# One PSUM pool of eight single banks, halves apart, and a new written order, in a memory-attention and spatial-gate kernel

## The chip, the cores and the metric

The kernel runs on one core of a Trainium2 chip. Its time is the device time of one execution in microseconds (us), the median of three runs. TensorE (PE in the profile) multiplies matrices and writes the products to PSUM, a memory of eight banks of 128 partitions by 512 fp32 values; VectorE (DVE) and ScalarE (ACT) read PSUM and write SBUF; GpSimd (POOL) works in SBUF alone; SyncE (SP) issues all DMA transfers here.

## The reference

For each of 8 batches (8 heads, 576 rows, 64 columns, 32 memories), `_attn_ref` makes memories out of the keys and values and lets the queries attend to them; `_moe_ref` puts the result through a gated layer whose gate mixes rows.

```python
a = softmax(phi)                                  # (b, h, 576, 32), over the memories
k_m, v_m = a^T k, a^T v                           # (b, h, 32, 64)
attn = softmax(q k_m^T / 8)                       # (b, h, 576, 32)
x = concat_heads(attn v_m)                        # (b, 576, 512)
h = relu(x w_in); u, v = halves of h              # 512 columns each
v_n = (v - mean) / sqrt(var + 1e-6)               # over the columns
v_s = w_spatial v_n + b_spatial[:, None]          # mixes the 576 rows
out = (u * v_s) w_out                             # (b, 576, 512)
```

`w_in` and `w_out` arrive in double precision, as pairs of 32-bit words that the kernel decodes.

## The kernel before, in words

Products that must be exact to fp32 are made of fp32r operands in two parts: a value x becomes hi = fp32r(x) and lo = x - hi, and a product is hi*hi + hi*lo + lo*hi, three matmuls. The low part is made by `low`: either DVE subtracts hi from x in PSUM, or PE adds minus hi onto x in its bank and ACT copies the rest out. ON_VECTOR names the ones that DVE makes; "wtl0" is one of them.

Each stage of a batch is a Python generator that yields after one or a few instructions, and each has a letter. P: exp(phi) and its sum (`memory_weights`). K: memories (`memories`, tiles kvm, tk, tv). Q: queries loaded and transposed. S: scores and their softmax (`scores`, tile sc, four banks). M0, M1: value memories times a half of w_in (`products`, tile mp, cast to mh and ml). V0 to V4: the gate half v of a tile of 128 rows (the last has 64), normalised (`gate`, tile pv). U0 to U3: the half u, transposed, for 128 of its 512 columns (`units`, tile pu, then one ACT Relu into u). G0 to G3: the row mixing for 128 columns (`spatial`, tile ps, 28 matmuls; then DVE multiplies by u into g, and ACT and DVE split g into gh, gl and the last 64 rows into grh, grl). O0 to O4: output rows (`project`, tile po, 12 matmuls, an ACT copy, a DMA). Once at the start: D loads w_in, E and L decode its two halves, X loads and decodes w_out, W loads w_spatial, T0 to T4 transpose it (tile wt), B adds the bias, and Z is an idle matmul that only keeps PE busy.

Nothing schedules these at run time. START, PLAN and END are strings of such letters, written by hand: each letter runs its generator up to its next yield, so the strings give the order of instructions on every engine and on every DMA queue. A prime means one batch ahead. START runs batch 0 and the first stages of batches 1 and 2, PLAN is walked for batches 1 to 5, END runs the last two. Each engine runs its own list in order and waits on the others by semaphores. A tile is given a bank of its pool when its first instruction is written, and where all banks of the pool are taken, that instruction waits for the last reader of the tile that gives way.

Before, PSUM is two pools: ps1, four single banks (`bank`), for mt, mb, kvm, tk, tv, sc, pv, po, tq, at and the idle matmuls; and ps2, two tiles of two banks each (`banks`), for wt, mp, pu and ps. So two of M, U, G can be in flight, and the third waits until the whole of a two-bank tile is read. A batch takes 9 to 10 two-bank tiles and some 19 single ones.

Of the kernel before, what the change touches and what calls it, by code (L numbers as in the profile page):

```python
# [26 lines left out]
    P'' G1 Q' K' V4 V3 X1 V2 V4 G1 G2*2 Q' V3 G2 K' V3 V4*2 P'' V3 K'*2 P'' G2 X1 Q' K' P'' G2
    X1 X3 P'' K'' G2 K' X2 G2 K'' K' G1 P'' X3 P'' X3 P'' G1 X3 G0 G1 G0 G1 K' G1*2 G0 P''*2 G0
    X2 G3 G2 K' P'' G3 X2 G2 S' M1' X2 G0 X2 P'' G3 G0*2 S'*2 O0 P'' X2 X3 G3 X2 X3 S' O2 X3 S'
    M1'*2 S' G3 G0 O3 G3 G0 G3 S' M1' O3 O1 S'*2 O3 P'' O1 P'' S' Q'' O1 S' G3 M1' S' G3 O0 S'  # L30
    O3 O2 S' M1' S' O0 S'*5 O2 K'' O0 K'' Q'' O2 O1 K''*2
# [6 lines left out]
    M1' K'' G1 S' G0 G1 P''' G0 S'*2 G1 G3 O1 S' G2 G1 S' M0 S' P''' G3 S'*2 G3 G0 G3 G2 O0 G3*2
    S'*2 G2 Q'' O2 G2 S' V1' G2 O1 V0' O3 V1' O1 V1' P''' O1 G2 O0 O1 V0' M1 O0 G2 K'' U3' Q''
    S' O3 V0' V4' O2 P''' Q'' O4 K'' Q'' O3 V4' O0 O4 V4' U1'*2 P''' O2 V4' O4 O2 O4 O0 V4' P'''  # L40
    K'' Q'' K''' O3
# [3 lines left out]
    V0 V1 V4 V1 V0 V1 K' U3*2 V0 V2 V0 U2 V2 U1 U2 V1 V3 V2*2 U2 V2 V3 U0*2 M0' U0 M1' Q' S' V4  # L45
    M0' V3 G1 M0'*2 M1' G1 V3 M0' M1'*2 V3 G0 M1' V2 V4 S' V2 V3 G0 G1 V4 S' G0 S'*2 V3 V4 S' G0
    S' G0 S' G1 G3 G0 G1 G0 S' G3 G1 G3 S' G3 S'*2 U1 G2 S' G2 G0 G1 G0 V4 G2*2 S'*3 G1 O3 S' G1
    G3 U1' S'*2 V0' V2' S' V1' G2 V0' U1' V1' U1' V0' O0 U0' O2 U0' U3' V2' G2 V3' U0' G3 V4 G2
    V1' V2' V0'*2 G3 O2 G2 V0' U2' V2' U2' V0' O0 V2' U3' U2' G3*2 V1' G0' V4' V1' V3' O3 V2'
    V1' V3' V1' V4' O0 G0' V3' V4' U3' G1' V3' V4' V2' V3' V4' O1 Q' G0' G2 G1' V3' V4'*2 O1 V4'  # L50
    Q' G1' O3 V4'*2 G1'*3 G0' G2' G1' G2'*2 G1' G0' G2' G0' G3' G0'*2 O1 G3' G0' G3'*2 O2 O0 O1'
    G3' O1 G3' G1' G2'*2 O4' O3' G2' O2 O0' G2' G3' O1'*3 O0' O3' G3' V4 O3' O3 O3' G2' G3' K'
    O0' O4' O0' O2' O4' O2'*2 O4' O2'
# [838 lines left out]
```

## Time and profile before

| | before |
|---|---|
| median of 3 runs | 436.64 us (435.97 to 437.99) |
| profiled execution, its own time | 436.06 us |
| its span, first to last instruction | 434.3 us |
| PE, DVE, ACT, POOL busy | 405.9, 275.1, 230.6, 102.5 us |
| matmuls | 3882 |

A profile of one execution gives each instruction's start and length on its engine, the idle time before it, and the engine that ended this idle time. The ends of matmuls are modelled and overlap the next one's start, so two neighbouring starts tell more of PE's rate than a length. PEld is the weight load, which runs beside PE. An idle time is put down to the releaser that came last.

### The profile page before, as it was taken

Reading aid. Unit: us, or ns where it says so; the run is one execution under the profiler, and the core shown is the slowest. Engines: PE = TensorE matmul, PEld = TensorE weight load, DVE = VectorE, ACT = ScalarE, POOL = GpSimd, SP = SyncE. Lnnn points to the kernel's source line nnn. Section 1 sums busy time; section 2 is a strip of 40 time slices with the busy share of each in tenths; the row PEclk is TensorE's granted clock in tenths of the full one; section 3 lists DMA queues with packets and bytes.
Section 4 is the critical chain, followed back from the end, with each engine's and each line's share of the span. In section 5 each row is a group of like instructions: output and inputs, shape, how many; then the busy total and the mean of one; then the engine's idle time right before and its main releaser. Section 6 shows DMA issues by size and latency. Waiting matters only on the chain.

```text
span 434.3 us, 9318 instructions
## 1 busy us (share of the span) xinstructions
PE 405.9 (93%) x3882; PEld 344.1 (79%) x3882; DVE 275.1 (63%) x492; ACT 230.6 (53%) x444; POOL 102.5 (24%) x191
## 2 busy tenths in 40 slices
...
GB/s 305 365 381 249 74 76 207 146 27 250 150 208 12 105 163 129 110 26 154 83 219 2 103 183 160 60 54 142 121 2 2 127 51 2 0 2 24 2 48 145
DMA packets 85725, 50.68 MB, mean 117 GB/s; under 512 B 66162, under 2 KB 70258, under 8 KB 85684
## 3 DMA queue, kind: packets, MB, share of 16 engines
...
q14 instruction: 11, 0.09, 0.1%
...
## 4 chain that ended last, share of the span: by engine, by line
PE 47%; DVE 20%; ACT 14%; DMA 8%; POOL 5%; issue 4%; SPq 1%; POOLq 0%; DVEq 0%; ACTq 0%
PE po L798 18%; PE ps L758 14%; PE pv L636 6%; PE pu L720 4%; ACT vr L693 4%; DMA raw<-in_moe_w_in_dram 3%; DVE ml L153 3%; DVE vl L698 3%; DVE rmx L553 2%; DVE sm L556 2%; ACT mh L612 2%; DMA out_dram<-o 2%; ACT vh L696 2%; DVE phi_sb L311 2%; DMA q_sb<-in_q_dram 1%
## 5 line engine op out<-in xcount | busy, mean ns | idle before, releaser
L758 PE MATMUL ps<-wth,vh 128*128 128x288 f32 x256 | 57.3, 305 | 7.4 <-DVE ml L153 4.1
L758 PE MATMUL ps<-wtl,vh 128*128 128x288 f32 x256 | 54.6, 294 | 0.0
L758 PE MATMUL ps<-wth,vl 128*128 128x288 f32 x256 | 54.5, 294 | 0.0
L758 PEld LDWEIGHTS ps<-wth,vh 128*128 128x128 f32 x256 | 40.8, 188 | 13.1 <-issue 4.4
L798 PE MATMUL po<-woh,gh 128*128 128x512 f32 x128 | 50.4, 394 | 0.2 <-DVE sm L547 0.2
L798 PE MATMUL po<-wol,gh 128*128 128x512 f32 x128 | 50.3, 393 | 0.0
L798 PE MATMUL po<-woh,gl 128*128 128x512 f32 x128 | 50.2, 392 | 0.0
L804 ACT COPY o<-po 128x512 f32<-128x512 f32 x36 | 21.1, 585 | 46.1 <-PE po L798 35.1
L758 PEld LDWEIGHTS ps<-wtl,vh 128*128 128x128 f32 x256 | 41.4, 188 | 0.0
L758 PEld LDWEIGHTS ps<-wth,vl 128*128 128x128 f32 x256 | 40.9, 188 | 0.0
L681 DVE BATCH_NORM_STATS2 st<-vr 128x6 f32<-128x512 f32 (+1 forms) x35 | 24.0, 684 | 22.9 <-ACT vr L678 22.8
L684 POOL TENSOR_SCALAR few<-few 128x1 f32<-128x1 f32 (+1 forms) x35 | 9.7, 276 | 120.1 <-DVE few L682 105.3
L693 ACT ACTIVATE vr<-vr,few 128x512 f32<-128x512 f32 (+1 forms) x40 | 32.5, 815 | 8.9 <-POOL few L688 8.9
L586 POOL CAST ar<-ah 128x128 fp32r<-128x128 f32 x7 | 6.1, 874 | 130.2 <-ACT ah L579 130.2
L433 DVE STREAM_TRANSPOSE qT<-q_sb 128x576 f32<-128x576 f32 x28 | 20.2, 753 | 23.6 <-DMA q_sb<-in_q_dram 19.0
L698 DVE TENSOR_TENSOR vl<-vr,vh 128x512 fp32r<-128x512 f32 x32 | 22.0, 691 | 20.5 <-ACT vh L696 19.6
L720 PE MATMUL pu<-ah,mh 128*128 128x288 f32 x128 | 28.9, 307 | 0.1
L579 ACT CAST ah<-aT 128x576 fp32r<-128x576 f32 x14 | 9.4, 675 | 36.3 <-DVE aT L575 36.3
L798 PEld LDWEIGHTS po<-woh,gl 128*128 128x128 f32 x128 | 24.1, 188 | 5.5
L153 DVE TENSOR_TENSOR ml<-mp,mh 128x512 fp32r<-128x512 f32 x28 | 18.8, 688 | 15.1 <-ACT mh L612 15.1
L798 PEld LDWEIGHTS po<-woh,gh 128*128 128x128 f32 x128 | 24.1, 188 | 5.1 <-issue 0.4
L720 PE MATMUL pu<-ah,ml 128*128 128x288 f32 x128 | 27.4, 296 | 0.4 <-ACT ml L151 0.4
...
## 6 DMA issues: line engine op xcount, KB each, us to landing
...
```

The lines of the kernel that those rows point to most:

```text
L153: nc.vector.tensor_tensor(lo, x, hi.bitcast(F32), op=ALU.subtract)
L433: nc.vector.transpose(qT[:, 2 * n : 2 * n + 2].rearrange("p h s -> p (h s)"), q_sb[:, 2 * n : 2 * n + 2].rearrange("p h i d -> p (h i d)"),)
L579: nc.scalar.copy(ah[:, r], aT[:, r])
L636: nc.tensor.matmul(pv, x[:, r, cs], m[:, r, DM:DFF], start=(n == 0), stop=(n == 5))
L681: nc.vector.bn_stats(st6, vr)
L684: nc.gpsimd.tensor_scalar_add(rs, mv[:, 1:2], 1e-6)
L693: nc.scalar.activation(vr, vr, AF.Identity, bias=sh, scale=rs)
L698: nc.vector.tensor_tensor(vl[:, st, :], vr, vh[:, st, :].bitcast(F32), op=ALU.subtract)
L720: nc.tensor.matmul(pu[:, hf, 0:HALF], m[:, r, cs], a[:, r, hf * HALF : (hf + 1) * HALF], start=(n == 0), stop=(n == 5),)
L758: nc.tensor.matmul(ps[:, hf, 0:HALF], a, w[:, hf * HALF : (hf + 1) * HALF], start=(n == 0), stop=(n == len(ops) - 1),)
L798: nc.tensor.matmul(po, a, w, start=(n == 0), stop=(n == 11))
L804: nc.scalar.copy(o, po)
```

## The change

- ps1 has eight single banks and ps2 is gone. The tiles pu, ps and mp become two single tiles each; the 576 columns of pu and ps stay cut in halves of 288.
- `units` runs its matmuls half by half (three for the first half, three for the second, in each of its two steps), and two Relu of 288 columns take the place of one of 576.
- `spatial` multiplies g in two halves, two DVE instructions in place of one.
- `transpose_spatial` has a tile for 512 columns and one for 64; each is cast and has its low part made apart. The names become wtl00, wtl01 and so on, so none is in ON_VECTOR: PE and ACT make the low part of tile 0 too.
- The tiles grh and grl are kept under the number of the pair of batches.
- START, PLAN and END are new throughout. In START w_spatial is loaded ahead of w_in, both pieces of w_in's second half ahead of its first half, and there are 29 idle matmuls where there were 25.

The diff; of the three strings the parts that the text below speaks of are shown.

```diff
--- before.py
+++ after.py
@@ -18,39 +18,41 @@
 PSUM = bass.MemoryType.PSUM
 
 START = """
-    P Z P*2 Z P*2 Q P*9 Q P Q P Q K Q*4 K Q*2 P Z Q Z Q Z D1 K W E0 K W K*2 Z D0 K*2 E0*2 Z K*4
-    S Z S K S*2 W S T1 D1 Z L0 S*2 T1 D0 Z X0 T4 Z T3 Z T3 S T1 S X1 T1 S E1 Z E0 S*3 Z T4 Z T4
-    T3 L0 Z S*2 L1 T3 E1 S Z T4 Z*2 T0 S E1 S T4 X1 Z E1 T0 S L0 L1 T0 S*2 Z M1*2 S*2 X1 L0 L1
...
+    P Q*2 Z P*2 K P*2 Q*2 P Q P*2 Q*2 P K Q P*2 Q*2 P Z Q P*4 K P K Q K*2 W K*3 Z*2 W K Z K T4 K
+    T0 D1 S T1 K D1 S D0 E0 Z T0 S*2 T0*2 S E0 S*2 T0 E0 Z W T1 S T1 Z*2 X0 D0 T4 Z T1 Z E1 Z E1
+    S T0 Z*2 S Z E0 Z*2 T3 Z T1 S T4 E1 X0 T1 S T3 L0 Z*2 E1 T4 T0 Z L1 L0 Z T1 S L1 L0 S T4 S
+    P' Z T3 S M1 X1 T3 Z T4 S M1 T3 T4 S*2 X1 Z*2 S*2 M1*2 X1 L1 T2 S*2 L0 L1 P' Z M1 T2 Z S Z
+    T2 S*3 M1 M0 T4 P' T2 V0 P' S P' X0 T2*2 M0 P' M0 T2 X0 P' V0 M0 P' M0 Q' V1 K' V0 V2 M0 V0
...
 """
 
 PLAN = """
-    M0 V0 V4 V1 V0 U1 U3 V2 V0 U3 U0 K' U0 V1*2 Q' P'' V2 V3 P'' V4 V0 V1 P'' U2*2 V3 S' V2*2 U0
-    M0' M1' V3 S' S S' P'' U2 P''*2 V2 K'' M0'*2 V3 M0'*2 M1'*2 K'' G1 M1' V3 G1 V2 V4 P'' M1'
-    P'' K''' S' G0*2 V3 V2 V4*2 G1 V3 P''' G0 S' G0 S' G1 G3 K'' S' G0 G3 S' G3 G0 G2*2 G1 K''*3
...
+    M0 V1 V4 V0 U0 V3 V1 K' V0 U0 V1 U1 P'' U3 U2 Q' U2 M1 V0 Q' P'' V1 V2 V0 U2*2 V3 U0 P'' S'
+    M0' V2 P'' V3 V2 S' V3 S' P'' V2 S' K'' P'' S' M0'*2 P'' M0' P'' M0' M0 V4 S' V3 M1' K''
+    G0*2 V2*2 V4 V3 G1 K'' V2 V3 P''' M1' V4*2 G1 M1' S' G1*2 S' G1 G0 K''' S G0 K'' P'''*2 G3
...
 """
 
 END = """
...
 """
 
 ON_VECTOR = set(
@@ -93,14 +95,10 @@
     one = ctx.enter_context(tc.tile_pool(name="one", bufs=1))
     three = ctx.enter_context(tc.tile_pool(name="three", bufs=3))
     two = ctx.enter_context(tc.tile_pool(name="two", bufs=2))
-    ps1 = ctx.enter_context(tc.tile_pool(name="ps1", bufs=4, space=PSUM))
-    ps2 = ctx.enter_context(tc.tile_pool(name="ps2", bufs=2, space=PSUM))
+    ps1 = ctx.enter_context(tc.tile_pool(name="ps1", bufs=8, space=PSUM))
 
     def bank(name):
         return ps1.tile([P, 512], F32, tag="b1", name=name)
-
-    def banks(name):
-        return ps2.tile([P, 2, 512], F32, tag="b2", name=name)
 
     ident = const.tile([P, P], F32, name="ident")
     make_identity(nc, ident)
@@ -234,14 +232,14 @@
             nc.gpsimd.tensor_copy(w_dup, w_sb[:, :, None, SM:S].to_broadcast([P, NI, 2, SR]))
             nc.gpsimd.tensor_copy(w_rem_dup, w_rem[:, None, SM:S].to_broadcast([SR, 2, SR]))
             yield
-        tp = banks(f"wt_{si}")
+        tp, tr = bank(f"wt_{si}"), bank(f"wr_{si}")
         for ti in range(NI + 1):
             if si < NI:
                 cols = (w_rem if ti == NI else w_sb[:, ti])[:, si * P : (si + 1) * P]
             else:
                 cols = (w_rem_dup if ti == NI else w_dup[:, ti]).rearrange("t c s -> t (c s)")
             n = cols.shape[0]
-            dst = tp[:, 0, ti * P : ti * P + n] if ti < NI else tp[:, 1, 0:n]
+            dst = tp[:, ti * P : ti * P + n] if ti < NI else tr[:, 0:n]
 
             nc.tensor.matmul(
                 dst,
@@ -252,14 +250,12 @@
                 stop=ti >= NI - 1,
             )
         yield
-        x = tp.rearrange("p a s -> p (a s)")[:, 0:S]
         hi = wth[:, si] if si < NI else ws1
-        nc.scalar.copy(hi, x)
-        yield
-        if si < NI:
-            yield from low(f"wtl{si}", wtl[:, si], x, hi)
-        else:
-            yield from low(f"wtl{si}", ws2[0:SR], x[0:SR], hi[0:SR])
+        lo, n = (wtl[:, si], P) if si < NI else (ws2[0:SR], SR)
+        for c, (cs, x) in enumerate(((slice(0, SM), tp), (slice(SM, S), tr[:, 0:SR]))):
+            nc.scalar.copy(hi[:, cs], x)
+            yield
+            yield from low(f"wtl{si}{c}", lo[:, cs], x[0:n], hi[0:n, cs])
 
     def prepare_bias(b, _):
 
@@ -596,8 +592,7 @@
         vT = state["vT", b]
 
         cs = slice(f * 512, (f + 1) * 512)
-        both = banks(f"mp_{b}_{f}")
-        mps = [both[:, r] for r in range(2)]
+        mps = [bank(f"mp_{b}_{f}_{r}") for r in range(2)]
         for j in range(NJ):
             for r in range(2):
                 nc.tensor.matmul(
@@ -711,25 +706,23 @@
             state["u", b] = one.tile([P, NJ, S], F32, name="u")
         u = state["u", b]
         (ah, al, _), (mh, ml) = state["a", b], state["m", b]
-        pu = banks(f"pu_{b}_{dt}")
         cs = slice(dt * P, (dt + 1) * P)
-        n = 0
+        pu = [bank(f"pu_{b}_{dt}_{hf}")[:, 0:HALF] for hf in range(2)]
+        at = [slice(hf * HALF, (hf + 1) * HALF) for hf in range(2)]
         for r in range(2):
-            for m, a in ((mh, ah), (mh, al), (ml, ah)):
-                for hf in range(2):
+            for hf in range(2):
+                for n, (m, a) in enumerate(((mh, ah), (mh, al), (ml, ah))):
                     nc.tensor.matmul(
-                        pu[:, hf, 0:HALF],
+                        pu[hf],
                         m[:, r, cs],
-                        a[:, r, hf * HALF : (hf + 1) * HALF],
-                        start=(n == 0),
-                        stop=(n == 5),
+                        a[:, r, at[hf]],
+                        start=(r == 0 and n == 0),
+                        stop=(r == 1 and n == 2),
                     )
-                n += 1
-            yield
-        nc.scalar.activation(
-            u[:, dt, :].rearrange("p (a s) -> p a s", a=2), pu[:, :, 0:HALF], AF.Relu
-        )
-        yield
+            yield
+        for hf in range(2):
+            nc.scalar.activation(u[:, dt, at[hf]], pu[hf], AF.Relu)
+            yield
 
     def spatial(b, dt):
         if ("g", b) not in state:
@@ -737,13 +730,13 @@
                 one.tile([P, NJ, SM], F32R, name=name) for name in ("gh", "gl")
             )
             if b % 2 == 0:
-                state["rem"] = tuple(
+                state["rem", b // 2] = tuple(
                     one.tile([P, NJ, 2 * SR], F32R, name=name) for name in ("grh", "grl")
                 )
-        u, (gh, gl), (grh, grl) = state["u", b], state["g", b], state["rem"]
+        u, (gh, gl), (grh, grl) = state["u", b], state["g", b], state["rem", b // 2]
         vh, vl, t1 = state["v", b]
         rc = slice((b % 2) * SR, (b % 2 + 1) * SR)
-        ps = banks(f"ps_{b}_{dt}")
+        ps = [bank(f"ps_{b}_{dt}_{hf}")[:, 0:HALF] for hf in range(2)]
         cs = slice(dt * P, (dt + 1) * P)
         ops = []
         for i in range(NI):
@@ -756,7 +749,7 @@
         for n, (a, w) in enumerate(ops):
             for hf in range(2):
                 nc.tensor.matmul(
-                    ps[:, hf, 0:HALF],
+                    ps[hf],
                     a,
                     w[:, hf * HALF : (hf + 1) * HALF],
                     start=(n == 0),
@@ -766,13 +759,10 @@
                 yield
         yield
         g = two.tile([P, S], F32, name="g")
-        nc.vector.tensor_tensor(
-            g.rearrange("p (a s) -> p a s", a=2),
-            u[:, dt, :].rearrange("p (a s) -> p a s", a=2),
-            ps[:, :, 0:HALF],
-            op=ALU.mult,
-        )
-        yield
+        for hf in range(2):
+            at = slice(hf * HALF, (hf + 1) * HALF)
+            nc.vector.tensor_tensor(g[:, at], u[:, dt, at], ps[hf], op=ALU.mult)
+            yield
         for hi, lo, x in (
             (gh[:, dt, :], gl[:, dt, :], g[:, 0:SM]),
             (grh[:, dt, rc], grl[:, dt, rc], g[:, SM:S]),
@@ -792,7 +782,7 @@
             if st < NI:
                 h_, l_ = (x[:, dt, st * P : (st + 1) * P] for x in state["g", b])
             else:
-                h_, l_ = (x[:, dt, :] for x in state["rem"])
+                h_, l_ = (x[:, dt, :] for x in state["rem", b // 2])
             woh, wol = (x[:, dt % 2] for x in state["wo", dt // 2])
             for a, w in ((h_, woh), (h_, wol), (l_, woh)):
                 nc.tensor.matmul(po, a, w, start=(n == 0), stop=(n == 11))
```

## Rows read from the trace of the kernel before

**Rows 1.** The page's part 1: busy time of an engine, its share of the span, and its instructions.

```profile
PE 405.9 (93%) x3882; PEld 344.1 (79%) x3882; DVE 275.1 (63%) x492; ACT 230.6 (53%) x444; POOL 102.5 (24%) x191
```

**Rows 2.** Busy time by stretch: from and to, its length, then busy time and instructions of PE, PEld, DVE, ACT and POOL, the granted clock of PE as a share of 2.4 GHz, the DMA engines' busy share and GB/s.

```profile
44.00:47.70 3.70, 3.52 (x20) 1.49 (x21) 2.93 (x5) 2.01 (x5) 2.47 (x3) 0.54 1.58 146
47.70:102.00 54.30, 52.56 (x616) 43.79 (x614) 37.26 (x65) 36.24 (x76) 19.03 (x35) 1.00 0.40 105
...
128.65:177.90 49.25, 48.01 (x464) 41.59 (x464) 32.84 (x61) 25.83 (x50) 9.62 (x21) 1.00 0.48 114
177.90:225.10 47.20, 45.38 (x452) 39.16 (x452) 32.64 (x61) 25.00 (x49) 10.22 (x21) 1.00 0.50 109
...
321.40:370.20 48.80, 46.04 (x317) 39.06 (x317) 29.99 (x55) 24.12 (x48) 6.78 (x17) 1.00 0.21 40
370.20:416.80 46.60, 46.53 (x293) 42.95 (x294) 22.54 (x43) 20.93 (x40) 8.55 (x17) 1.00 0.05 18
```

**Rows 3.** What PE waited for in the whole span: the tile it was to write or read and its line, the releaser, us in total, how often, the longest.

```profile
PE ps L758 <- DVE ml L153: 4.1, 5, 1.3
PE mt L296 <- DVE mx L283: 3.9, 2, 3.6
PE ps L758 <- DVE g L769: 2.7, 6, 0.9
...
PE mb L305 <- ACT cmb L302: 2.2, 3, 0.8
...
PE pv L636 <- ACT vr L678: 1.1, 1, 1.1
...
PE mp L603 <- DVE g L769: 0.6, 1, 0.6
...
PE mp L603 <- ACT u L729: 0.4, 1, 0.4
PE pv L644 <- ACT o L804: 0.3, 1, 0.3
PE po L798 <- DVE sm L547: 0.2, 1, 0.2
```

**Rows 4.** PE's timeline at one batch boundary: start, length, line, tile and operands, shape, how many in a row, and the idle time before it with its releaser.

```profile
211.03 1.20 PE L536 MATMUL sc<-qT,kT 64*32 64x288 f32 x32
212.03 2.05 PE L603 MATMUL mp<-win_sb,vT 64*32 64x512 f32 x32
213.87 2.22 PE L338 MATMUL kvm<-kv_sb,phi_sb 64*32 64x128 f32 x144
216.73 0.51 PE L758 MATMUL ps<-wth,vh 128*128 128x288 f32 x2 [0.64 <-DVE ml L153]
...
224.04 0.69 PE L758 MATMUL ps<-ws,t 128*128 128x288 f32 x4
225.09 0.53 PE L758 MATMUL ps<-wth,vh 128*128 128x288 f32 x2 [0.35 <-DVE g L769]
```

**Rows 5.** The end of the chain of waits: start, length, and so many matmuls in a row.

```profile
405.95 10.84 PE ps L758 x82
416.79 13.74 PE po L798 x60
```

**Rows 6.** Instructions grouped by line and form: engine, operation, tile, shape, count, busy us and mean ns of one, and the idle time before them.

```profile
L769 DVE TENSOR_TENSOR g<-u,ps 128x576 f32<-128x576 f32 x32 | 23.2, 742 | 5.7 <-PE ps L758 5.5
L782 DVE TENSOR_TENSOR gl<-g,gh 128x512 fp32r<-128x512 f32 x32 | 22.2, 708 | 8.3 <-ACT gh L780 8.2
L729 ACT ACTIVATE u<-pu 128x576 f32<-128x576 f32 x32 | 20.5, 644 | 5.1 <-PE pu L720 4.9
L678 ACT ACTIVATE vr<-pv 128x512 f32<-128x512 f32 x28 | 16.6, 594 | 18.6 <-PE pv L636 17.5 <-DVE vl L698 1.1
L547 DVE STREAM_TRANSPOSE sm<-sc 128x288 f32<-128x288 f32 x28 | 12.2, 460 | 0.0
L681 DVE BATCH_NORM_STATS2 st<-vr 128x6 f32<-128x512 f32 x28 | 19.2, 684 | 17.0 <-ACT vr L678 16.9
L782 DVE TENSOR_TENSOR grl<-g,grh 128x64 fp32r<-128x64 f32 x32 | 6.7, 208 | 8.9 <-ACT grh L780 8.9
L311 DVE TENSOR_TENSOR phi_sb<-phi_sb,mb 128x1152 f32<-128x1152 f32 x7 | 9.5, 1352 | 3.2 <-PE mb L305 3.2
L383 ACT COPY vT<-tv 128x128 f32<-128x128 f32 x8 | 2.1, 264 | 0.0
```

**Rows 7.** GpSimd's timeline in the start: the decoding of w_in and what it waits for.

```profile
17.32 2.89 POOL L178 TENSOR_SCALAR raw<-raw 128x1024 int32<-128x1024 uint32 x1 [14.68 <-DMA raw<-in_moe_w_in_dram]
...
28.19 7.01 POOL L178 TENSOR_SCALAR raw<-raw 128x1024 int32<-128x1024 uint32 x2 [0.84 <-DMA raw<-in_moe_w_in_dram]
```

**Rows 8.** VectorE's timeline in the start, its first and its last instruction ahead of the second product of w_in.

```profile
24.35 0.69 DVE L480 TENSOR_REDUCE rmx<-sc 128x16 f32<-128x512 f32 x1 [2.88 <-PE sc L451]
...
42.32 1.22 DVE L186 SCALAR_TENSOR_TENSOR win_sb<-raw 128x1024 int32<-128x1024 int32 x1
```

**Rows 9.** PE's timeline up to the first pv: the last low part of the scores, the product M0 and the first matmul of pv.

```profile
44.18 0.44 PE L142 MATMUL at<-ah,minus 128*128 128x128 f32 x1 [0.60 <-ACT ah L519]
44.60 1.96 PE L603 MATMUL mp<-win_sb,vT 64*32 64x512 f32 x16
46.50 0.79 PE L636 MATMUL pv<-mh,ah 128*128 128x512 f32 x1
```

More of the change, by code (lines that the diff above doesn't have):

```diff
@@ L20 @@
 START = """
-    P Z P*2 Z P*2 Q P*9 Q P Q P Q K Q*4 K Q*2 P Z Q Z Q Z D1 K W E0 K W K*2 Z D0 K*2 E0*2 Z K*4
-    S Z S K S*2 W S T1 D1 Z L0 S*2 T1 D0 Z X0 T4 Z T3 Z T3 S T1 S X1 T1 S E1 Z E0 S*3 Z T4 Z T4
-    T3 L0 Z S*2 L1 T3 E1 S Z T4 Z*2 T0 S E1 S T4 X1 Z E1 T0 S L0 L1 T0 S*2 Z M1*2 S*2 X1 L0 L1
-    P' S M1 L1 P' X0 P' T2 Z X0*2 M1 B S M1 B Q' K' S P' M1 S T2 P' M0 S V0 M0*2 V0 T2 P' Z V4
-    M0 P'*3 V2 V1 V0 Z T2 M0 V4 X1 U1 P' X0 P' V0*2 X0 V0 M0 V1 V0 P' V3 P' M0 U1 V2 V4 V1 X0 K'
-    P' V4 U0 P' V2 U1 U0 K' Q' K' V4 U0 V1*2 V2 V1 U2*2 V2 Q' V1 U3 Z U3 U2 V3 V4 G1 V2 V3 U3
@@ L27 @@
[L27 to L31, printed above, removed]
+    P Q*2 Z P*2 K P*2 Q*2 P Q P*2 Q*2 P K Q P*2 Q*2 P Z Q P*4 K P K Q K*2 W K*3 Z*2 W K Z K T4 K
@@ new lines @@
+    T0 D1 S T1 K D1 S D0 E0 Z T0 S*2 T0*2 S E0 S*2 T0 E0 Z W T1 S T1 Z*2 X0 D0 T4 Z T1 Z E1 Z E1
+    S T0 Z*2 S Z E0 Z*2 T3 Z T1 S T4 E1 X0 T1 S T3 L0 Z*2 E1 T4 T0 Z L1 L0 Z T1 S L1 L0 S T4 S
+    P' Z T3 S M1 X1 T3 Z T4 S M1 T3 T4 S*2 X1 Z*2 S*2 M1*2 X1 L1 T2 S*2 L0 L1 P' Z M1 T2 Z S Z
+    T2 S*3 M1 M0 T4 P' T2 V0 P' S P' X0 T2*2 M0 P' M0 T2 X0 P' V0 M0 P' M0 Q' V1 K' V0 V2 M0 V0
+    X0*2 V2 M0 Q' V1 P'*2 T3 V2 X1 K' V3 P' V1 P' V1 U1 U3 V0 P' X0 U3 U1*2 U2 U3*2 U2 P' X1 U1
+    V0 V1 V4 K' V2 K' X3 U2 T3 V0 P' V1 X1 V3 V1 V4 V2 U2 G0 Q'*2 K' V4 V3 K' G1 Q' V2 K' V4 K'
@@ L32 @@
+    U0 P'' G0 U0 G1 X1 G2 V2 K' V3 P'' V4 V3 V4 B V3*2 V4 X2 G1 K'' G2 G0 U0 G2 B V4*3 K' G2 X2
+    U0 Q' G2 K' G2 G1 K' G1 K' X3 G2 G1 X3 S' M1' G2*2 K'' X3 X2 S'*2 G1 G0 X2 G2 P'' G0 G3 G0
+    X3 G0 X3 Q'' P'' X2 G0 P'' G0 G3 G0 X3 G1 G3 X2 S' G3 P'' G3 S' G3 O1 O2 G3 S' M1'*2 P''*2
+    O3 P'' O0 G3 G1 X2 G3 O1 S' G1 O2 G3 S' Q'' P'' S' M1' S' P'' O1 P'' O0 K'' S' K'' S'*2
+    P''*2 S'*2 M1' O3 P'' O1 S'*2 M1' O2*2 S'*2 K'' O3 O0 K'' S' O3 O0
 """
 PLAN = """
-    M0 V0 V4 V1 V0 U1 U3 V2 V0 U3 U0 K' U0 V1*2 Q' P'' V2 V3 P'' V4 V0 V1 P'' U2*2 V3 S' V2*2 U0
@@ L36 @@
-    M0' M1' V3 S' S S' P'' U2 P''*2 V2 K'' M0'*2 V3 M0'*2 M1'*2 K'' G1 M1' V3 G1 V2 V4 P'' M1'
-    P'' K''' S' G0*2 V3 V2 V4*2 G1 V3 P''' G0 S' G0 S' G1 G3 K'' S' G0 G3 S' G3 G0 G2*2 G1 K''*3
[L38 to L41, printed above, removed]
+    M0 V1 V4 V0 U0 V3 V1 K' V0 U0 V1 U1 P'' U3 U2 Q' U2 M1 V0 Q' P'' V1 V2 V0 U2*2 V3 U0 P'' S'
@@ new lines @@
+    M0' V2 P'' V3 V2 S' V3 S' P'' V2 S' K'' P'' S' M0'*2 P'' M0' P'' M0' M0 V4 S' V3 M1' K''
+    G0*2 V2*2 V4 V3 G1 K'' V2 V3 P''' M1' V4*2 G1 M1' S' G1*2 S' G1 G0 K''' S G0 K'' P'''*2 G3
+    G2 G1 G3 G0 G2 G0 S' P''' S'*3 M1' K'' G0 Q'' P''' K'' S' G1 G2 S' G0 S' G2 G0 G1 G3*2 M1 G1
+    S' K'' O2 G1 G2 P''' G0 S' G3 S' G3 O1 M1' O0 G2 S' V0' G3 G2*2 S' G3 O0 O1 K''' O0 V4' O4
+    O0 O2 O1 G3 O3 V1' V0' O2 V0' O0 V4' G2 G3 K'' Q'' U1' V4' U3' V4' U3' G2 K'' V1' O4 O2 V1'
+    O1 V4' O3 K'' O4 U1' O1 U3' O3 U1' P''' O4 Q''*2 O3 U0'
@@ L42 @@
 """
 END = """
[L45 to L53, printed above, removed]
+    V0 V1 U1 V1 U2 Q' V0 U1 V0 V2 U3 V4*2 V1 U0 V0 V4 K' V3 U0 V1 Q' U3 V2 U0 U2 V3 U0 M0' V4*3
+    U2 S' V3*2 U2 V2 S' G1 V2 S' G1 S'*2 M0'*2 V3 V2*2 U3 S' V2 M1'*2 V3 M1' G0 S' M1' G0 S' G0
```

8 lines of the change are left out of this document (added).

## The prediction

> **What bounds the kernel now.** I read the busy times first. PE is busy 93% of the span, DVE 63%, ACT 53% [rows 1]: this is a kernel of matmuls, and the question is what PE does in the rest. Its rate comes from rows in which nothing holds it: 82 ps matmuls of 288 columns in 10.84 us, 132 ns each, and 60 po matmuls of 512 columns in 13.74 us, 229 ns each [rows 5]. Per batch there are 112 ps and 48 pu matmuls (160 x 0.132 = 21.1 us), 54 po on average and 28 pv (82 x 0.229 = 18.8 us), and sc, mp and kvm one after the other, from 211.03 to 213.87 + 2.22 = 216.09 (5.1 us) [rows 4]. With about 1 us for ten small transposes a batch can't go below some 46 us, and two neighbouring batches take 49.25 and 47.20, 48.2 in the mean [rows 2]. So the steady part has 2 us a batch to give, whatever is done about PSUM, and the stretch from 370 us on has nothing: 46.53 busy of 46.60.
>
> The waits of PE come next [rows 3]. Nearly all of them are waits for a bank, told by releasers that only read PSUM: ps behind ml (4.1 us) and behind g (2.7), mp behind g and u (0.6 and 0.4), pv behind vr and o (1.1 and 0.3), po behind sm (0.2): 9.4 us in 5 + 6 + 1 + 1 + 1 + 1 + 1 = 16 waits. The timeline shows them return at one place of every batch [rows 4]. Two mp tiles hold both two-bank tiles, the first ps must have the first of them and waits 0.64 us until DVE has read its second half; some 8 us on, ps waits 0.35 us for g. A wait costs more than its idle time, since the end of a matmul is modelled late: four ps from 224.04 would let the next start at 224.04 + 4 x 0.132 = 224.57, and it starts at 225.09, so 0.52 us are gone where the row says 0.35. With 0.16 us on each of 16 the banks cost 9.4 + 2.6 = 12.0 us. What is left over are chains of data: mb behind cmb (2.2) and mt behind mx (3.9, nearly all of it the first 7 us) [rows 3].
>
> **The change part by part.** *Eight single banks.* It can take away up to 12.0 us, and takes nothing where a wait only passes on. I go through the new boundary in the written order. From mb on PE has V2's pv (6 x 0.229 = 1.37), sc (1.00), M0 (16 of 32 matmuls in 1.84, so 0.92), the first 80 of 144 kvm (1.23) and then M1 [rows 4, 5]: 4.5 us to M1. sc, M0 and kvm take 4 + 2 + 2 = 8 banks, so M1 gets the first two that sc gives back. Ahead of that DVE has one vl (0.71, as for gl), the subtraction on phi (1.35), two statistics (1.37) and two transposes out of sc (0.92) [rows 6]: 4.35 us. That is a tie. G0's first ps comes at 4.5 + 0.92 + 0.99 = 6.4 us and takes sc's other banks, free at 5.3; G1's takes M0's, 1.58 us later, and DVE and ACT have two halves to split for that from 5.3 on. So the wait behind ml goes with about 1 us to spare, and a small wait of M1 behind sm is late next. The waits behind g become waits for halves, and the first half is free some 0.28 us earlier (742 less 458 ns, below). Bounds: 0 and -12.0 us. I take 60%, -7.2, since two of three places have room and one is tied.
>
> *More instructions.* A Relu of 512 columns out of PSUM takes 594 ns and a copy of 128 takes 264 [rows 6], so 288 columns take 264 + 160 x 330/384 = 401 ns, and two take 803 where one of 576 took 644: 32 x 0.16 = 5.1 us more on ACT. On DVE 512 columns take 708 and 64 take 208, so 288 take 458, and two 916 against 742: 32 x 0.17 = 5.6 us more. Beside them lies PE's own work, with DVE at 63% and ACT at 53% [rows 1]; without that cover the price is 5.6 us, where each g stands on the path of a ps. The first g half can also begin before the second half's matmuls, which gives 0.13 us back each time. Bounds: -4 and +5.6; I take +0.5, since of 32 g only some six held PE up [rows 3]. The pu matmuls keep their number and each its own weight load, so I take nothing for their order; three in a row into one bank are what po and pv do at full rate [rows 5]. The state under the pair's number moves no instruction.
>
> *START.* The first pv stands at 46.50 behind M0, which starts at 44.60 behind the low part of the scores [rows 9]. M0 needs all of w_in's first half, and the last piece of that is loaded later now. By the shapes 10.2 MB stand ahead of its end (phi 0.59, three of q, k, v 1.18 each, w_spatial 1.33, three other pieces of w_in 1.05 each, one of w_out 0.52, and itself), where 5.2 MB were in at 17.3 us [rows 7]; so it lands near 34 us, GpSimd takes 3.5 more (7.01 for two), and DVE can merge it from 37.5. But DVE's own list is longer: its 23 instructions of softmax and decoding from 24.35 on ended at 42.32 + 1.22 = 43.54 [rows 8], 19.2 us. The new list has one merge more there (1.22) and no wtl0 (0.74, as g's 576 columns): 19.7 us, to 44.0. And it puts four merges ahead of the end of the softmax, 4.9 us; that end came eight instructions of some 1.1 us ahead of 43.54, near 34.5, and would now come near 39.4. Ten casts and low parts of some 0.59 us [rows 6] follow it on ACT, and M0 stands behind them: 45.9 or so, 1.3 us later than 44.60. Against that, PE ran at a granted 0.54 from 44.0 to 47.7 [rows 2]: M0 took 1.96 us where 16 matmuls take 0.92 at the full clock [rows 4, 9]. If four more idle matmuls keep it busy, 1.0 to 1.5 us come back. wtl0's low part goes to PE, two small matmuls where it idles. SP issues batch 1's v behind four query transfers instead of two; the first use of v stands well behind the first pv. Bounds: -2 and +3; I take +0.5, about what is left of the two.
>
> *The rest of the order.* mb and mt now stand elsewhere in PE's list; their data chains may gain or lose what they cost now, -1.5 to +1.5 [rows 3]. I take 0.
>
> **The sum.** 436.06 - 7.2 + 0.5 + 0.5 = 429.9 us for the profiled execution. That one lies 0.58 below the median of the runs, so I say 430.4 for the median.
>
> **The rivals.** *The waits only pass on.* With one pool every tile stands behind every other, and M1's tie becomes the wait that ps had. For it speaks the tie of 4.5 against 4.35 us; against it, that G0 and G1 have 1 us or more in hand. Then about 436.6.
>
> *DVE falls behind at the boundary; slower.* The place is M1 and the first ps, which take the banks of sc, and sc is read by four DVE transposes behind two statistics and the subtraction. Before, sc had its own four banks and mp and ps didn't depend on it. The price is what DVE is late beyond the tie, at each of seven boundaries. Before, a boundary lost 0.64 + 0.16 behind ml and 0.52 behind g, 1.3 us [rows 4]; where DVE is later than that, the change loses. At 2.1 us late it is 7 x 0.8 = 5.6 us slower with nothing gained elsewhere: 442. For it: the longest of these instructions come in front of sc's. Against: DVE is busy 32.6 of 47.2 us a batch [rows 2].
>
> *START is late by its bound.* +3 in place of +0.5: 433.
>
> *More goes than I take.* Ten of the 12 us go and the stretch at 0.54 with them: 425 or a little less, 424.
>
> *The clock falls between the batches.* After 47.7 us the granted clock is 1.00 in every stretch, with waits of up to 1.3 us at every boundary [rows 2, 3]. If each of six boundaries had a stretch as from 44.0 to 47.7, it would lose 3.7 x 0.46 = 1.7 us, 10 us in all: 441. The Trainium skill, "TensorE: Matmul & The Clock Gate", section "A second HAM failure mode: psum-queue depth-cycling", says that a kernel that went through the PSUM banks in a circle let PE idle for so short times, so often, that its clock went up and down. Going through all eight banks is what the change does; the trace of before, which goes through four and two, shows none of it.
>
> **How the numbers follow.** Forecast 430.4, chance 0.46; its own range is 425 to 434. Waits pass on: 0.17. DVE behind: 0.14. START late: 0.09. More goes: 0.10. Clock: 0.04. A measurement of this kernel can tell about 0.5% (2.2 us) from no change, so faster is below 434.4: the forecast, START late (most of it) and more goes, 0.46 + 0.07 + 0.10 = 0.63. Same: 0.17 + 0.02 = 0.19. Slower: 0.14 + 0.04 = 0.18. The range of 8 in 10 runs from 423, which leaves out a complete success with START at its better bound, to 441, which leaves out half of the slower cases.
>
> **What would show it.** Right, if PE waits for ps behind ml and behind g are below 3 us together, if PE's waits that end in a reader of PSUM sum to some 4 us instead of 9.4, if a batch takes 47 us, and if ACT and DVE are each 5 us busier. If M1 waits behind sm by 1 us or more a batch, the waits have passed on or DVE is behind; the mean batch, below or above 48.2, tells which. The first pv later than 48 would be START. A granted clock below 1.00 after 60 us would be the clock. The prediction is wrong if the steady batch stays at 48 us.

## The result, and the profile after

The changed kernel takes 420.8 us (median of 4 runs, 420.19 to 422.0) against 436.9 us in the same rounds: a ratio of 0.963, with a 95% interval of 0.960 to 0.967. The forecast was 430.4 with a range of 423 to 441. The kernel is faster than the lower end of that range: the gain is 16 us where 6 were forecast.

| | before | after |
|---|---|---|
| span of the profiled execution | 434.3 us | 419.0 us |
| PE busy | 405.9 us (93%) | 399.5 us (95%) |
| first pv starts | 46.50 us | 48.61 us |
| sc of batch 2 starts | 114.61 us | 112.58 us |
| last matmul ends | 430.52 us | 415.27 us |

The page's part 1 of the kernel after, against [rows 1]:

```profile
PE 399.5 (95%) x3888; PEld 343.9 (82%) x3888; DVE 273.1 (65%) x523; ACT 233.1 (56%) x487; POOL 95.3 (23%) x191
```

What PE waits for in the kernel after, the whole list, against [rows 3]:

```profile
PE tq L394 <- DMA q_all<-in_q_dram: 8.2, 1, 8.2
PE sc L447 <- issue: 1.9, 1, 1.9
PE wt L244 <- issue: 1.8, 1, 1.8
PE wt L140 <- ACT wth L256: 0.9, 1, 0.9
PE kvm L334 <- DMA kv_sb<-in_v_dram: 0.7, 1, 0.7
PE mt L292 <- DVE mx L279: 0.7, 1, 0.7
PE kvm L334 <- issue: 0.6, 1, 0.6
PE at L140 <- ACT ah L515: 0.4, 1, 0.4
PE tk L366 <- ACT kmn L353: 0.3, 1, 0.3
PE mp L140 <- ACT mh L607: 0.2, 1, 0.2
```

Not one row is left of ps behind ml or g, mp behind g or u, pv behind vr or o, po behind sm, and mb behind cmb is gone with them. All but mt (at 83 us), the low part of mp (0.2, at 86.5) and kvm behind issue (0.6, at 302) belong to the first 50 us. The windows of four steady batches, cut at similar places as in [rows 2], have no idle PE either, bar 0.6 us in the last:

```profile
126.00:174.00 48.00, 48.00 (x468) 41.93 (x467) 33.58 (x68) 26.31 (x55) 9.17 (x21) 1.00 0.46 112
174.00:219.00 45.00, 45.00 (x457) 39.81 (x457) 33.27 (x66) 25.60 (x53) 9.17 (x21) 1.00 0.54 117
219.00:266.00 47.00, 47.00 (x463) 41.30 (x463) 32.52 (x65) 25.78 (x53) 9.15 (x21) 1.00 0.51 118
266.00:311.00 45.00, 44.39 (x450) 38.93 (x449) 31.66 (x63) 25.44 (x52) 9.17 (x21) 1.00 0.51 88
```

From sc of batch 2 (112.58) to sc of batch 6 (296.84) are 184.3 us, 46.1 a batch; before it was 307.31 - 114.61 = 192.7, 48.2 a batch. 46 was the floor that the prediction estimated from matmul rates, so the steady part now runs at about what PE can do. The boundary that [rows 4] show looks like this:

```profile
205.15 1.20 PE L532 MATMUL sc<-qT,kT 64*32 64x288 f32 x32
206.14 1.06 PE L598 MATMUL mp<-win_sb,vT 64*32 64x512 f32 x16
207.00 1.33 PE L334 MATMUL kvm<-kv_sb,phi_sb 64*32 64x128 f32 x79
...
208.95 1.16 PE L334 MATMUL kvm<-kv_sb,phi_sb 64*32 64x128 f32 x64
210.04 0.54 PE L751 MATMUL ps<-wth,vh 128*128 128x288 f32 x2
210.41 0.43 PE L751 MATMUL ps<-wtl,vh 128*128 128x288 f32 x2
```

M1 (left out, at 208.09) stands between the two parts of kvm, and the first ps starts 4.89 us after sc with no idle time before it; it was 5.70 us (216.73 - 211.03).

### The profile page after: what moved, and what is told of

Same layout as the page of the kernel before. It is cut to its first block, busy times and chain, and to the rows that moved or that the text cites. A ratio compares the mean times of both kernels' runs of the same rounds, so it can differ in the third digit from the quotient of the medians.

```text
span 419.0 us, 9410 instructions
## 1 busy us (share of the span) xinstructions
PE 399.5 (95%) x3888; PEld 343.9 (82%) x3888; DVE 273.1 (65%) x523; ACT 233.1 (56%) x487; POOL 95.3 (23%) x191
## 4 chain that ended last, share of the span: by engine, by line
PE 91%; DMA 3%; DVE 2%; issue 2%; ACT 1%; SPq 0%; ACTq 0%; DVEq 0%
PE ps L751 28%; PE po L788 23%; PE pu L715 12%; PE pv L631 11%; PE kvm L334 4%; PE mp L598 3%; DMA kv_sb<-in_v_dram 3%; PE idle L807 2%; PE sc L532 2%; PE pv L647 1%; PE pv L639 1%; PE sc L447 1%; PE wt L244 1%; PE wt L140 1%; PE tk L366 1%
## 5 line engine op out<-in xcount | busy, mean ns | idle before, releaser
L751 PE MATMUL ps<-wth,vh 128*128 128x288 f32 x256 | 56.3, 301 | 0.0
L693 DVE TENSOR_TENSOR vl<-vr,vh 128x512 fp32r<-128x512 f32 x32 | 23.0, 724 | 30.4 <-ACT vh L691 30.2
L715 PE MATMUL pu<-ah,mh 128*128 128x288 f32 x128 | 38.3, 299 | 0.0
L715 PE MATMUL pu<-al,mh 128*128 128x288 f32 x128 | 37.8, 295 | 0.0
L715 PE MATMUL pu<-ah,ml 128*128 128x288 f32 x128 | 37.6, 294 | 0.0
L679 POOL TENSOR_SCALAR few<-few 128x1 f32<-128x1 f32 (+1 forms) x35 | 8.3, 238 | 115.6 <-DVE few L677 102.3
L764 DVE TENSOR_TENSOR g<-u,ps 128x288 f32<-128x288 f32 x64 | 26.3, 441 | 12.4 <-PE ps L751 11.9
L770 ACT CAST gh<-g 128x512 fp32r<-128x512 f32 x32 | 19.8, 619 | 25.4 <-DVE g L764 25.3
L724 ACT ACTIVATE u<-pu 128x288 f32<-128x288 f32 x64 | 25.6, 418 | 5.6 <-PE pu L715 4.1
L582 POOL CAST ar<-ah 128x128 fp32r<-128x128 f32 x7 | 2.6, 373 | 113.1 <-ACT ah L575 113.1
```

The lines of the kernel that those rows point to most:

```text
L693: nc.vector.tensor_tensor(vl[:, st, :], vr, vh[:, st, :].bitcast(F32), op=ALU.subtract)
L715: nc.tensor.matmul(pu[hf], m[:, r, cs], a[:, r, at[hf]], start=(r == 0 and n == 0), stop=(r == 1 and n == 2),)
L724: nc.scalar.activation(u[:, dt, at[hf]], pu[hf], AF.Relu)
L751: nc.tensor.matmul(ps[hf], a, w[:, hf * HALF : (hf + 1) * HALF], start=(n == 0), stop=(n == len(ops) - 1),)
L764: nc.vector.tensor_tensor(g[:, at], u[:, dt, at], ps[hf], op=ALU.mult)
```

## Experiments

Eleven runs: nine new kernels, one of them (e1) run twice, and the changed kernel once more (e7). Beside the median I give the stretch from the start of batch 2's sc to the end of the last matmul in the profiled execution, since the start of a run varies by 1 to 2 us with the loads: two profiles of one kernel (e1) had the first pv at 46.02 and at 44.77.

| kernel | median us | ratio to before (95%) | sc of batch 2 to the end, us |
|---|---|---|---|
| before | 435.9 to 436.9 | | 315.9 |
| e9_halves_only | 437.0 | 1.001 (0.999 to 1.003) | 315.5 |
| e8_readers_apart | 430.6 | 0.987 (0.984 to 0.990) | 310.2 |
| e4_split_banks | 427.2 | 0.977 (0.972 to 0.982) | 308.4 |
| e1_old_order, e1_again | 424.8, 425.3 | 0.975, 0.976 (0.971 to 0.978) | 305.5, 305.2 |
| e5_end_only | 425.4 | 0.974 (0.971 to 0.978) | 306.5 |
| e9_mb_later | 426.5 | 0.978 (0.976 to 0.981) | 307.8 |
| e3_new_start_only | 423.8 | 0.973 (0.969 to 0.977) | 305.0 |
| e2_old_start | 421.9 | 0.969 (0.964 to 0.973) | 303.6 |
| e6_two_moves | 421.6 | 0.966 (0.963 to 0.969) | 302.9 |
| changed kernel, e7_changed_again | 420.8, 421.2 | 0.963, 0.965 (0.960 to 0.968) | 302.7, 302.7 |

**The banks without the order, the order without START, START alone.** Each is the changed kernel with strings of before: e1_old_order with all three, e2_old_start with START, e3_new_start_only with PLAN and END. Where a string is that of before, the two halves of a Relu and of g (and, with START of before, the two parts of a transposed tile) are written at the one place that it has for them:

```diff
-            yield
+            yield hf == 0
...
-        next(threads[key], None)
+        while next(threads[key], None) and state["together"]:
+            pass
```

> The changed code with the written order of before: eight single banks, halves apart, but START, PLAN and END as they were; both halves of u, of g and of each transposed tile stand where the one instruction stood. Theory A, the pool and the halves take the bank waits away by themselves: PE's waits behind ml and g fall from 6.8 to under 2 us and the time is 424 to 428 us. Theory B, the order does it and the pool only gives it room: two pairs written one after the other still wait for the reader that is written between them; the waits stay above 5 us and the time is 434 to 438 us.

> The changed kernel with START as before (halves and casts at its old places), PLAN and END new. The first pv came at 48.61 instead of 46.50 us in the changed kernel. If the new START simply costs these 2.1 us, this runs at 418 to 419.5 us, below both kernels. If START pays them back later (the first boundary came 4.5 us sooner after the first pv than before), it runs at 421 to 424 us.

> The changed kernel with its new START, PLAN and END as before. Theory A (pool and halves do it): some 425 to 429 us, e1 and at most 2 us more. Theory B (the order does it): 433 to 438 us, since only the part before 102 us runs in the new order.

e1 took 424.8 us: the pool and the halves bring 11.4 us of the 16, with the order of before word for word. Among what PE still waits for in it (second profile) are 2.5 us that the whole change no longer shows, one chain of data and one wait for a bank:

```profile
PE mb L304 <- ACT cmb L301: 1.6, 3, 0.7
PE ps L754 <- DVE ml L149: 0.9, 2, 0.7
```

e2, with the new PLAN and END on top, took 421.9 us, 2.9 less than e1 by the medians. From sc of batch 2 on, its profile is 1.6 to 1.9 us shorter than e1's two (table), so the order is worth some 2 to 3 us. e3, with the new START on top, took 423.8, some 1 less than e1 and below the range of either theory. START's 1 us is at the edge of what the intervals tell apart, and e2 shows why it is so little. In e2 the first pv starts at 43.82, 4.8 us ahead of the changed kernel, and sc of batch 2 is only 0.9 us ahead (111.68 against 112.58). Part of the 4.8 us is no lead, since the new START has done other work ahead of its first pv: sc of batch 1 starts at the same time in both (75.22 and 75.23), with some 20 ps more done in e2, 2.8 us. Most of what is then lost goes in two waits between 102 and 107 us, here in e2:

```profile
103.37 0.59 PE L370 MATMUL tk<-ident,kmn 128*128 128x128 f32 x2 [0.60 <-ACT kmn L357]
106.74 0.33 PE L296 MATMUL mt<-ident,mx 128*128 128x128 f32 x1 [0.77 <-DVE mx L283]
```

The second of them is a wait for a load. mx waits for the next phi_sb to land at 104.88, which SP issued at 99.72, behind output rows that wait for their o:

```profile
99.72 0.39 SPq L288 DMA_DIRECT2D phi_sb<-in_phi_dram  x1
```
```profile
104.88 0.69 DVE L277 TENSOR_TENSOR half<-phi_sb 128x512 f32<-128x512 f32 x1 [1.42 <-DMA phi_sb<-in_phi_dram]
```

In the changed kernel that load is issued at 100.24, hardly later, though its pv started 4.8 us later: it too stands behind the outputs. So a good part of what the early pv wins is waited away there.

**The halves without the banks.**

```diff
-        nc.scalar.activation(u[:, dt, :]..., pu[:, :, 0:HALF], AF.Relu)
+        for hf in range(2):
+            nc.scalar.activation(u[:, dt, at], pu[:, hf, 0:HALF], AF.Relu)
...
+        for hf in range(2):
+            nc.vector.tensor_tensor(g[:, at], u[:, dt, at], ps[:, hf, 0:HALF], op=ALU.mult)
```

> The kernel before with nothing but the Relu and the product g cut in two halves; two-bank tiles and order as before. It prices the 64 more instructions. The prediction took +0.5 us with bounds of -4 and +5.6. If the chain behind g ends waits of PE, +1 to +4 us; if they lie beside other work, within 1 us of before; DVE and ACT each about 5 us busier in any case.

437.0 us, 0.6 us above before by the ratio, with an interval that holds 1. PE still waits for ps behind ml and behind g, as in [rows 3]:

```profile
PE ps L758 <- DVE ml L153: 3.8, 5, 1.3
PE ps L758 <- DVE g L771: 2.9, 6, 1.0
```

The halves alone take neither wait away, and their 64 more instructions cost about nothing. (In e1 and e4 the matmuls of pu also run half by half; this order was not run alone.)

**Two rings of four in place of one of eight.** This leaves single banks and halves, but keeps the old division of PSUM. The edit, against e1_old_order:

```diff
-    ps1 = ctx.enter_context(tc.tile_pool(name="ps1", bufs=8, space=PSUM))
+    ps1 = ctx.enter_context(tc.tile_pool(name="ps1", bufs=4, space=PSUM))
+    ps2 = ctx.enter_context(tc.tile_pool(name="ps2", bufs=4, space=PSUM))
...
-        mps = [bank(f"mp_{b}_{f}_{r}") for r in range(2)]
+        mps = [half(f"mp_{b}_{f}_{r}") for r in range(2)]    # ps2; also wt, wr, pu, ps
```

> As e1_old_order (halves, single banks, the three orders of before), but the eight banks in two rings of four: one for the tiles that were single before (sc, mt, mb, kvm, pv, po, idle), one for the halves (wt and wr, mp, pu, ps). Theory A, sharing: ps of the next unit needs both its halves within 0.13 us of its start, so banks that come back one at a time help little; what helped in e1 is that the halves may take any bank of eight. Then the waits come back: 432 to 436 us, PE behind ml 3 to 4 us and behind g 2 to 3 us. Theory B, one bank at a time: a half's bank comes back when its own reader is done, 0.4 us (u, g) or 0.6 us (ml) before the pair's, and that is enough: 424 to 428 us, PE behind ml under 1.5 us and behind g under 0.5.

427.2 us, and PE shows no wait of ps behind ml at all: the time of theory B. But a half of ps follows the other within 0.13 us, so a bank that comes back sooner than its neighbour can't be worth much. The readers of mp tell what it was. ScalarE's casts and VectorE's subtractions at one boundary of the kernel before:

```profile
213.96 0.56 ACT L612 CAST mh<-mp 128x512 fp32r<-128x512 f32 x1
215.28 1.07 ACT L612 CAST mh<-mp 128x512 fp32r<-128x512 f32 x2 [0.76 <-DVE ml L153]
217.22 0.59 ACT L612 CAST mh<-mp 128x512 fp32r<-128x512 f32 x1 [0.87 <-DVE ml L153]
```
```profile
214.55 0.69 DVE L153 TENSOR_TENSOR ml<-mp,mh 128x512 fp32r<-128x512 f32 x1 [1.15 <-ACT mh L612]
215.90 1.29 DVE L153 TENSOR_TENSOR ml<-mp,mh 128x512 fp32r<-128x512 f32 x2 [0.65 <-ACT mh L612]
217.84 0.69 DVE L153 TENSOR_TENSOR ml<-mp,mh 128x512 fp32r<-128x512 f32 x1 [0.65 <-ACT mh L612]
```

and the same in e4:

```profile
210.28 2.03 ACT L614 CAST mh<-mp 128x512 fp32r<-128x512 f32 x4
```
```profile
210.87 2.48 DVE L153 TENSOR_TENSOR ml<-mp,mh 128x512 fp32r<-128x512 f32 x4 [1.15 <-ACT mh L614]
```

Before, the cast of a pair's second half waited until VectorE had read its first half. The two halves share no data; they were only one tile. Four casts and four subtractions took from 213.96 to 218.53, 4.57 us; apart they take 3.07. Over the whole run ScalarE stood 10.8 us in 14 such waits, in a row of the kernel before that the prediction didn't read, since it looked only at what PE waits for:

```profile
ACT mh L612 <- DVE ml L153: 10.8, 14, 0.9
```

What two rings leave and one ring of eight takes away are the waits behind g. Here is such a place in e4, where the second of two ps (from 220.01) has its weight load wait for g:

```profile
219.43 0.69 PE L758 MATMUL ps<-ws,t 128*128 128x288 f32 x4
220.01 0.77 PE L758 MATMUL ps<-wth,vh 128*128 128x288 f32 x2
220.61 0.44 PE L758 MATMUL ps<-wtl,vh 128*128 128x288 f32 x2
```
```profile
220.37 0.19 PEld L758 LDWEIGHTS ps<-wth,vh 128*128 128x128 f32 x1 [0.18 <-DVE g L771]
```

From 219.43 to 220.61 are 1.18 us for six matmuls of 0.132 us, 0.79 in all: 0.4 us is lost. The kernel before lost 0.6 us at its place by the same count, from 224.04 [rows 4] to

```profile
225.46 0.44 PE L758 MATMUL ps<-wtl,vh 128*128 128x288 f32 x2
```

Over the six such places of a run the loss is 4.3 us in the kernel before, 2.4 in e4 and nothing in e1 (second profile).

**The readers' order alone**, in the kernel before, with its pairs of banks:

```diff
+        lows = [low(f"ml{b}{f}{r}" if b < 2 else None, ml[:, r, cs], mps[r], mh[:, r, cs]) for r in range(2)]
         for r in range(2):
             nc.scalar.copy(mh[:, r, cs], mps[r])
             yield
-            yield from low(f"ml{b}{f}{r}" if b < 2 else None, ml[:, r, cs], mps[r], mh[:, r, cs])
+            if b < 2:
+                yield from lows[r]
+        if b >= 2:
+            for r in range(2):
+                yield from lows[r]
```

> The kernel before, with its pairs of banks; only the order in which the four readers of a pair mp are written is changed, from batch 2 on: both casts mh on ScalarE, then both subtractions ml on VectorE, in place of mh, ml, mh, ml. In the kernel before ScalarE waits 0.76 and 0.87 us for ml between its casts and VectorE 0.65 for each cast, although the second cast reads the other half of the pair: the four take 4.57 us where they take 3.07 in e4_split_banks. Theory A, readers on two engines take turns at one tile: ScalarE's waits behind ml go from batch 2 on, ml of the first pair ends 5.3 us after the start of sc in place of 5.54 and ml of the second 6.5 in place of 7.5, so ps starts 0.2 us earlier and the gap of 0.27 before its second pair closes: 0.5 us a boundary, over five or six of them 2.4 to 2.9 us, 433.0 to 434.0 us. Theory B, the waits are for the bank alone, or come from the data of mh: the waits of ScalarE behind ml stay, and the time stays at 435.5 to 436.8.

430.6 us, 5.5 less than before with not one bank changed. ScalarE's wait behind ml shrinks from 10.8 us to 1.0 (batches 0 and 1). The turns themselves stay: the four casts now run in a row, and VectorE's first subtraction begins when the second cast is done, 1.08 us after the first began, where in e4 it begins 0.59 after it.

```profile
212.39 2.02 ACT L613 CAST mh<-mp 128x512 fp32r<-128x512 f32 x4
```
```profile
213.47 2.48 DVE L153 TENSOR_TENSOR ml<-mp,mh 128x512 fp32r<-128x512 f32 x4 [1.63 <-ACT mh L613]
```

The time fell by twice what I had reckoned. PE's waits of ps behind ml go from 4.1 to 2.8 us, those behind g from 2.7 to 0.3. Counted from start to start as above, the places behind g lose 1.3 us in place of 4.3, so some 3 of the 5.5 us came back there, at a place that the edit doesn't touch.

**Where the order's 2 to 3 us lie.** e5 has START and PLAN of before and END of the change.

> The changed kernel with START and PLAN of before and END new, so e1_old_order with the order of the last two batches changed. From e1_old_order to e2_old_start (PLAN and END new) the median fell by 2.9 us. Theory A, END carries it: its 120.0 us from the fifth boundary to the last matmul become about 118.7: 422.5 to 424.0 us. Theory B, PLAN carries it (five batches, with the wait of mb behind cmb, 1.7 us, and of ps behind ml, 0.9 us, in them): END alone leaves 424.3 to 425.3 us, and those two waits of PE stay.

425.4 us, the same as e1 (425.3), and mb's waits are there (2.3 us): END brings nothing by itself. The two waits of ps behind ml that e1 has in END are gone, and two others of 0.44 us stand in their place (pv behind vT at 345 us, ps behind u at 354). So what e2 gains over e1 needs the new PLAN as well.

The starts of sc say where it is gained. From sc of batch 2 to sc of batch 6, e1's two profiles take 185.4 and 185.3 us and e2's 184.9. From there to the last matmul e1 takes 120.0 in both, e5 120.5 and e2 118.8. So 1.2 of the 1.6 to 1.9 us lie in the last walk of PLAN and in END, and with END alone (e5) they don't come. The two waits of mb that PLAN has in e1 stand ahead of that, in a stretch that differs by 0.6 us at most.

Then mb and the subtraction behind it were moved by hand in the old PLAN:

```diff
-    ... Q' P'' V2 V3 P'' V4 V0 V1 P'' U2*2 V3 S' ...
+    ... Q' P'' V2 V3 V4 V0 V1 U2 P''*2 U2 V3 S' ...
```

> e1_old_order with one step of PLAN moved: mb (and the subtraction behind it) is written after the first half of the pu of unit 2 in place of before it, 0.8 us of matmuls later. Theory A: what the new PLAN brings over the old one is mostly this wait (mb behind cmb, 1.7 us in three waits, up to 0.9 us each), and it goes: 1.2 to 1.8 us under e1_again, 423.0 to 423.6 us. Theory B: it is passed on, to exp of phi_sb and kvm behind it, or to sc: within 0.5 us of e1_again, with a new wait behind phi_sb or ml.

> e1_old_order on the chip and in the rounds of e9, to read a difference of 0.3%: 424.8 us by its first runs, 424.2 to 425.6, with waits of mb behind cmb of 1.7 us and of ps behind ml of 0.9 us.

e9_mb_later took 426.5 us, 1.2 more than e1_again, where one theory said 1.2 to 1.8 less and the other the same within 0.5. mb's waits fell from 1.6 to 0.9 us (0.7 of either in the first 10 us), and another came in their place: mb takes its bank later, and in one ring the tiles behind it then stand behind other readers. The second product of a boundary now waits for a Relu, which e1_again doesn't show:

```profile
161.31 1.20 PE L535 MATMUL sc<-qT,kT 64*32 64x288 f32 x32
162.31 1.06 PE L601 MATMUL mp<-win_sb,vT 64*32 64x512 f32 x16
163.54 1.39 PE L601 MATMUL mp<-win_sb,vT 64*32 64x512 f32 x16 [0.16 <-ACT u L727]
164.42 2.53 PE L337 MATMUL kvm<-kv_sb,phi_sb 64*32 64x128 f32 x144
166.88 0.53 PE L754 MATMUL ps<-wth,vh 128*128 128x288 f32 x2
```

sc to the first ps are 5.57 us here and 4.89 in e1_again (161.34 to 166.23). That is the rival "the waits only pass on", in one ring and by one move. What the new PLAN does better than the old was not found.

**Two steps of the changed kernel.** mt at 83 us and a low part at 86.5 had the only waits of PE between 50 and 300 us.

```diff
-    ... X2 S' G3 P'' G3 S' G3 O1 O2 G3 S' M1'*2 P''*2 O3 P'' O0 ...
+    ... X2 S' G3 G3 S' G3 O1 P'' O2 G3 S' M1' P''*2 O3 M1' O0 P'' ...
```

> The changed kernel with two steps of START written later, near 83 us: the transpose mt of batch 2 behind the next six po matmuls (1.4 us of work), and the low-half matmul of mp behind six more; mb of batch 2 goes behind O0 with it. In the changed kernel PE stood 0.69 us before that mt and 0.24 before that mp, 0.86 and 0.40 from start to start. Theory A: TensorE has no other limit there and the time falls by the sum, 1.0 to 1.3 us, to 419.5 to 419.9 us, with both waits gone and the first sc of the second boundary 1.0 to 1.3 us earlier than 112.58. Theory B: as with e2_old_start, what is won in START is handed back by the loads of the next batch (phi_sb is one buffer, free when kvm has read it): 420.6 to 421.2 us, and the second boundary's sc within 0.3 us of 112.58 or a new wait behind phi_sb before 110 us.

> The changed kernel itself, on the chip and in the rounds of e5 and e6, so that a difference of 0.3% can be read: 420.8 us by its first runs, 420.0 to 421.6.

421.6 against 421.2 us: nothing. Both waits are gone, sc of batch 2 starts at 112.55 against 112.48, and PE waits elsewhere: 0.31 us for gl at 83.9, and gaps at kvm near 97 and at tk near 105.7 that the changed kernel has not. So theory B, in small pieces. No version here beats the changed kernel.

## Why the prediction was wrong

*What bounds the kernel: right.* PE's rate and the floor of 46 us a batch held to 0.1 us (46.1), and the place of the loss was the batch boundary.

*"I take 60%, -7.2": the term that failed first.* The bank waits were worked out as 12.0 us. With the old order, e1 is 10.8 to 11.4 us faster than before, and e9_halves_only puts the halves' price at 0.6: the banks gave 11.4 to 12.0, as much as the whole bound. The 40% that I left to a tie of M1 with sm didn't come: no wait of mp behind sm stands in e1 or in the changed kernel. That the gain equals the bound is in part luck. e1 (second profile) still has 1.6 us of such waits (ps behind ml 0.9, mp behind g 0.5, po behind sm 0.2), so those that went were worth more than I had added up. And the cause that I gave was half right. I read "ps behind ml" as a wait for a bank that comes back late, and the one pool of eight as its cure. e8 shows that 5.5 us lie in turns that two engines take at one tile, with no bank changed; e4 (8.7 us below before) that cutting the tiles, without one pool, takes every wait of PE behind ml. One pool takes some 2 us more: the medians' intervals overlap, but the places behind g lose 2.4 us in e4 and nothing in e1.

*"The rest of the order: I take 0": wrong by 2 to 3 us.* e1 to e2 is 2.9 us by the medians and 1.6 to 1.9 from sc of batch 2 on, and needs the new PLAN too (e5: END alone gives none). I looked at the waits of mb and mt alone. The wait of mb behind cmb, 2.2 us [rows 3], is gone in the changed kernel, but it can't be the main cause: 0.7 of it stands at 8 us and stays in e2, the stretch with the other two differs by 0.6 us at most between e1 and e2, and moved alone it was passed on. Most of the gain lies behind sc of batch 6. Which step gives it stays open.

*START: +0.5, measured about -1, hardly told from no change.* Both terms were there:

```profile
47.59 1.09 PE L598 MATMUL mp<-win_sb,vT 64*32 64x512 f32 x16
48.61 0.50 PE L631 MATMUL pv<-mh,ah 128*128 128x512 f32 x1
```

M0 starts 3.0 us later than before, where the term for the cast chain said 1.3, and it runs at the full clock (1.09 us against 1.96), as the counter-term said. So the first pv comes 2.1 us later, and later than 48, which I had named as the sign of a late START; yet the time didn't rise. What I missed is that the place where pv starts sets little: with the new PLAN, sc of batch 2 comes at 111.7 to 112.6 with either START, and in e2 a wait for the next batch's phi_sb stands between.

*The halves: +0.5, measured +0.6.* The sizes, g and u of 288 columns in the changed kernel, against 458 and 401 ns that I interpolated from [rows 6]:

```profile
L764 DVE TENSOR_TENSOR g<-u,ps 128x288 f32<-128x288 f32 x64 | 26.3, 441 | 12.4 <-PE ps L751 11.9
L724 ACT ACTIVATE u<-pu 128x288 f32<-128x288 f32 x64 | 25.6, 418 | 5.6 <-PE pu L715 4.1
```

That is 5.1 us more on ACT and 3.1 on DVE by these groups. The page's busy times don't show it (ACT +2.5, DVE -2.0), so "each 5 us busier" was a poor sign to name.

*The sum.* Some 4.5 us of banks, 2 to 3 of the order and 1.5 of START are 8 to 9 of the 9.6 that the forecast missed.

*The rivals.* "More goes than I take" came nearest, with 0.10 and 424 us, and was still 3 us short. "DVE falls behind at the boundary" and "waits only pass on" fall for this change; e9_mb_later and e6 show the second at work elsewhere. The clock: granted 1.00 in the four steady windows above with all eight banks in the circle. So what the Trainium skill ("TensorE: Matmul & The Clock Gate", section "A second HAM failure mode: psum-queue depth-cycling") says of a clock that goes up and down does not show here; the short, frequent idle times of PE that it speaks of are hardly left.
